# Softmax sums: turned by VectorE, written to DRAM in rows and read back for both heads at once, with a new instruction order

## The chip, the cores and the metric

The kernel runs on one core of a Trainium2 chip. The metric is device time in microseconds (us) of one execution, as the median of several runs.

## The reference

Attention with a threshold, for 4 batches, 8 heads, 576 queries and keys and a head width of 64, and behind it two feed-forward blocks over the 2304 resulting rows of 512:

```python
scores = (q @ k.T) / 8
thresh = max(scores) - tau                      # per query
scores = where(scores >= thresh, scores, -1e9) - max(scores)
attn = exp(scores)
attn = attn / (sum(attn) + 1e-9)                # one sum per query and head
x = (attn @ v) -> rows of 512                   # [2304, 512]
h = x @ w_in                                    # [2304, 2048]
g = (a0 + a1*h + a2*h**2 + a3*h**3) / (1 + |b0|*|h| + |b1|*h**2 + 1e-6)
y = g @ w_out                                   # [2304, 512]
out = ((y @ w1) * (y @ w2)) @ w3 @ w_out2       # [2304, 512]
```

## The kernel before

Two heads are worked on together as a pair: the 64 values of head 0 lie in partitions 0 to 63, those of head 1 in partitions 64 to 127. A unit of attention is a batch `b`, a pair `c` (0 to 3) and a half `u` of the queries: `u` = 0 is two blocks of 128 queries, `u` = 1 two more and the last 64 queries of both heads in one block (`blk` 4). There are 32 units. In a unit TensorE makes the scores (`qk`, L484 to L502), VectorE the maxima (`top`), ScalarE or VectorE the exponentials with their sums (`exp`), each block of probabilities is split into two 16-bit parts (`p_hi`, `p_lo`: tile `hl`) and transposed by a DMA (`p_t`, L584: `pT`, `pL`), and TensorE multiplies by the values (`pv`, L599).

The sums come out one per partition (one partition is one query), but they are needed along the free axis, because `pv` leaves the result with the queries along the free axis. So `recip` takes a unit's sums (tile `su`, 128 partitions by 4 or 5 columns: a column is a block and a head), adds 1e-9, takes the reciprocal (L552, L553, VectorE) and writes them to a buffer in DRAM, `d_r` (L555). `spread` reads them back, copied to 64 partitions for each head, into tile `R` (L563 for the 256 queries of both blocks, one DMA for each head; L567 for the 64 of `blk` 4, again one for each head). `x_split` (L610) and `x_tail` (L624) multiply the result of `pv` by `R`; this gives `xp` and `xl`, the input of the first feed-forward block.

That block (`mlp1`, tiles of 128 rows) runs `h_product` (L813), the rational function on ScalarE, VectorE and GpSimd (`act_h`, `num`, `den`, `inv`, `quotient`), a DMA transpose (`turn`, L865: `gt`) and `y_product` (L877). The second (`mlp2`) runs `ab_product` (L984), `c_mul`, a DMA transpose (`turn`) and `o_product` (L1013), and stores (`o_store`, L1025). Weights are loaded and split into 16-bit parts between (L675, `conv_w`, `split_w`).

All DMAs are issued by SyncE (SP), in one queue and in the order of the program. An instruction on SP that has to wait holds all that stand behind it. The order of the whole program is a written-out list, `ORDER`: each token is an event's number (a function call with its arguments; each time that it stands there the event goes on to its next `yield`), a letter for the engine of a step that can run on several (`a` ScalarE, `p` GpSimd, none or `v` VectorE), and the buffers that it takes. A planner outside the kernel made the list. Each engine works its part of the list strictly in order.

Of the kernel before, what the change touches and what calls it, by code (L numbers as in the profile page):

```python
# [10 lines left out]
F32 = mybir.dt.float32  # L11
# [5 lines left out]
ALU = mybir.AluOpType  # L17
# [14 lines left out]
0 5.0 1.1 3.2 12.0.1 19.2.3 2.0.0 7.1 4.1 13a 10.2 6.0 23.0.1 15.0 21p 25.0 8.1 27 22.1 9 29a.0  # L32
9.0 31.0.4 9 33.5 31v 11v.0.0 35a.6 33v 48.0.1 38p 17a.1.1 42p.7 40.0 11 44v 18.2 17 46.1 24.0
50.1 52 41.0 24 54v.1 24 56.8 86.4.0 20.1 34.1 58.1 20 56a 20 58a 90.0.1 60v.5 26.2 63v 73 65 43.2
67v.6 43 69v 73 43 71 92.2 88p 94 36.3 14.0 96v.2 36 98.1.7 36 100.8 152.1.5 28.4 98a 28 100a
115.0.1 28 75.0 108v.6 30.1 102p.3 37.2 117.3 119 104p 154a 121p.0 16.5 106.2 123.2 111v 125.7 16
123v 16 127a.8 32.6 45.0 125v 156.0.1 129p 140 140 39.7 32 39 131 32 39 49.1 159.0 134p.2 72.2 161
136p 163v.1 165.2.3 47.8 167.8 47 165a 47 167a 182.0.1 169p.7 59.0 51.9 171p 175p.3 53.1 51 74.10
51 74 62.1 61.11 74 53 61 81.2 177v 61 53 184.1 99.0 64.12 186 53 64 188p.2 190.0 64 192.4 77.0.0
190v 76.1 83a.2.2 55v.13 192v 219.0.1 113.0 194a.8 83 200a.6 101.14 80.1 173.1 79 101 79v 101  # L40
112.2 80 79v 116.0 78.15 138 196v 78 66.0 207 202p 221.2 207 198 223 66 78 225a.0 227.0.0 114.16
114 85.1 215.7.4 80 227v 114 118.17 89.2 66 118 232a.2 209.1 118 142.0 234v 80 230.8 598.0 230v 66
82a.18 238v.0 87.19 240v 107.1 87 217v 87 281 103.1 107 91.20 68v.21 244.0.1 91 93.0 91 246.3
# [12 lines left out]
332.6 273.1 636 280 352a 243 332v 243 334a.1 339 245p.0 251a.49 424.0 339 336p 424 356.0.1 264a.50
297.1 272a.51 424 253a.52 275 254a.53 424 253.0 275v 338.6 424 268a.54 275p 264.1 249a.55 358.3
274a.56 253v 341.1 260a.8 258v.9 251.0 280 264a 360 256a.10 249.1 304.2 251v 247a.11 319 361v.2
262a.15 254.0 249v 266a.12 260.1 270a.14 373.19 373 254v 363.2.7 260v 365.8 247.0 373 363a 306.20
256.1 284.0 365a 247v 306 266.0 256v 372p.1 378.0.1 306 266v 374p 311.2 444.0 380.0 381 268.1  # L60
286.23 383a.0 367v.4 387.5 286 272.0 387a 268v 426.1 286 272v 298.0 313.22 274.1 293.16 313 258.0
293 274v 426 258v 293 444 313 428.0 317.1 324.2 300.30 430 262.1 446.1 300 430 270.0 262v 400.1
385.8 385a 300 270v 331.0 302.1 443 448 375.0 320.17 428.1 448 428.0 320 347.1.1 376.0 433v 320
435 326.5 337.1 322.0 333.1 326 435 333 437.0 326 437 351.2 329.0 333 309.0 437 357.0 335.0 340.0
446.0 349 437p 401.1 446.1 461.1 349a 403p.1 340 439.0 405.3 353.4 276a.26 340 405a 353 344.1
343.0 450v 461 394a.1 359.3 452 353 445.0.1 452 359 364.2 355.1 455.1 342.1 359 315.1 455 377.0
463.0 346.6 455 466 349p 455v 466 457.1 366.24 346 379.7 346 379 664.1 348.1 366 362.0 379 282.1
366 431.0 463.0 423.2 447.2 463.0 449 289.1 468v 295.1 412 368.1 345.0 412 369v 470 345v 407v.6
370.2 382.1 345v 396v 470 384 389p.7 451a.2 398 384.1 508.0 453.0.5 409p 384 453a 414.0 386p.1
413a.2 399p.28 388a.40 508 411.3 417a.35 456a.4 410p.29 417.1 393p.36 276.0 417v 391v 440.1.6  # L70
388.1 472.0 392 454.8 276v 479.1 454a 390v.39 408a.33 406v.38 479 395v.43 388a 472 458v 410.0
481.1 472 481.1 390.1 442p 410v 510.0 483 472p 393.0 462a.5 512 481.1 390v 467.0.1 475.2 425.1.0
512 393a 441.1 483 510.0 427.2 469.3 510.0 420.1 460.1 486v 464v 488 395.0 471 514p 488 465.0 422
473v.0 636.0 416.1 395v 476.7 516.0.8 636 517 441 490.1 644a.41 422v 517 490 399.0 656a.46 476v
639p.0 650a.45 525.0 399v 484p.3 415a.37 418 490 642a.42 644.0 485v 419a.44 525 648a.24 422v 487
644v 490p 402a.47 397a.48 413.0 418p 492.0 418v 661a.6 489.1 653a.23 413v 404a.16 666.30 402.0
491.0 520 429.1 666 528.1 675.2 402v 658a.22 666 406.0 474.4 493v.1 686.1 530 669.1 474v 406a
672.1 495.5 530 404.0 518a 478v.7 495a 678.21 480v 522.0.1 678 482 404v 678 408.0 688.4 746.2
681.1 524.1 683 408a 688 432.1 397.0 502 688 502 434.0 526 696.1 397a 527v.2 529.1.2 648.0 529a
# [196 lines left out]
def tile_attention_mlps(  # L276
# [16 lines left out]
    nc = tc.nc  # L293
# [948 lines left out]
```

## Time and profile before

| | |
|---|---|
| median of 3 runs | 1327.58 us (1326.79 to 1328.59) |
| the profiled execution's own time | 1328.86 us |
| its span, from the first to the last instruction | 1327.1 us |
| mean granted clock of TensorE over the span | 0.911 of full speed |
| TensorE (PE) busy with matmuls | 1044.2 us, 79% |
| VectorE (DVE) busy | 874.2 us, 66% |
| ScalarE (ACT) busy | 584.1 us, 44% |
| GpSimd (POOL) busy | 339.2 us, 26% |

The own time is what the device counted for the profiled execution; the span is what its records cover, and the 1.8 us between the two lie outside of the instructions. Busy times are sums over the instructions of an engine. "SPq" is SyncE's sequencer, which issues the DMAs.

### The profile page before, as it was taken

Reading aid. Unit: us, or ns where it says so; the run is one execution under the profiler, and the core shown is the slowest. Engines: PE = TensorE matmul, PEld = TensorE weight load, DVE = VectorE, ACT = ScalarE, POOL = GpSimd, SP = SyncE. Lnnn points to the kernel's source line nnn. Section 1 sums busy time; section 2 is a strip of 40 time slices with the busy share of each in tenths; the row PEclk is TensorE's granted clock in tenths of the full one; section 3 lists DMA queues with packets and bytes.
Section 4 is the critical chain, followed back from the end, with each engine's and each line's share of the span. In section 5 each row is a group of like instructions: output and inputs, shape, how many; then the busy total and the mean of one; then the engine's idle time right before and its main releaser. Section 6 shows DMA issues by size and latency. Waiting matters only on the chain. (4 is left out here: it accounts for less than half of the span.)

```text
span 1327.1 us, 15744 instructions
## 1 busy us (share of the span) xinstructions
PE 1044.2 (79%) x5281; PEld 487.8 (37%) x5284; DVE 874.2 (66%) x1690; ACT 584.1 (44%) x1067; POOL 339.2 (26%) x353
## 2 busy tenths in 40 slices
PE   2388657577767969777798876787988989889998
PEld 1133323233323434343344333343434434444443
DVE  6566879877673767757575755675966754647652
ACT  4221365665642455453454544644643434425520
POOL 1201121211211333333331321253341423211210
PEclk9999778797888988898998897889998999999999
DMA  8789595675883868597578867477475445852333
GB/s 231 143 175 205 194 166 171 136 126 143 122 167 59 129 88 151 92 142 135 102 129 81 142 99 112 74 176 85 93 139 110 89 102 90 101 61 56 57 63 71
DMA packets 365345, 159.47 MB, mean 120 GB/s; under 512 B 329936, under 2 KB 342224, under 8 KB 365264
## 3 DMA queue, kind: packets, MB, share of 16 engines
q1 hardware_dynamic: 365264, 158.47, 65.3%
q8 instruction: 41, 0.67, 0.3%
q14 instruction: 40, 0.33, 0.1%
HBM read 74.71 MB, written 8.20 MB: 62 GB/s over the span
## 5 line engine op out<-in xcount | busy, mean ns | idle before, releaser
L877 PE MATMUL y<-wp,gt 128*128 128x512 f16 x864 | 221.3, 409 | 64.5 <-DMA gt<-gg 62.2
L813 PE MATMUL h<-wp,xp 128*128 128x512 f16 x768 | 185.1, 391 | 13.8 <-DVE R L610 10.1
L984 PE MATMUL h<-wp,yy 128*128 128x512 f16 x576 | 143.7, 400 | 24.4 <-DVE R L624 7.1
L877 PEld LDWEIGHTS <-gt 128*128 128x128 f16 x864 | 87.1, 104 | 189.1 <-DMA gt<-gg 71.8
L502 PE MATMUL S<-raw 64*128 64x288 f32 x512 | 101.2, 474 | 50.3 <-ACT p L539 18.5
L346 POOL TENSOR_TENSOR hl<-p,hl 128x576 f16<-128x576 f32 x71 | 99.4, 1403 | 140.7 <-ACT hl L330 68.0
L511 DVE TENSOR_REDUCE m<-S 128x1 f32<-128x576 f32 x144 | 104.1, 748 | 36.4 <-PE S L502 27.4
L813 PEld LDWEIGHTS <-xp 128*128 128x128 f16 x768 | 75.4, 100 | 112.1 <-issue 32.7
L1013 PE MATMUL y<-wp,gt 128*128 128x512 f16 x432 | 104.6, 390 | 9.4 <-DMA gt<-gg 9.4
L984 PEld LDWEIGHTS <-yy 128*128 128x128 f16 x624 | 62.5, 102 | 113.3 <-issue 43.2
L821 ACT ACTIVATE U<-h,cf 128x512 f32<-128x512 f32 x72 | 55.8, 775 | 88.4 <-PE h L813 45.0
L346 POOL TENSOR_TENSOR A<-A,r 128x512 f32<-128x512 f32 x40 | 52.8, 1321 | 156.1 <-ACT r L828 146.0
L534 ACT ACTIVATE S<-S,th 128x576 f32<-128x576 f32 x90 | 62.2, 711 | 68.3 <-DVE th L353 38.5
L502 PEld LDWEIGHTS S<-raw 64*128 64x128 f32 x512 | 55.3, 206 | 93.5 <-issue 44.0
L737 PE MATMUL y<-cw,dg 128*128 128x512 f32 x112 | 63.8, 653 | 29.4 <-DVE wp L334 20.3
L334 POOL CAST hl<-p 128x576 f16<-128x576 f32 x45 | 33.7, 751 | 189.2 <-DVE p L537 47.0
L346 POOL TENSOR_TENSOR gg<-A,r 128x512 f16<-128x512 f32 x37 | 51.7, 1397 | 116.6 <-DVE A L856 61.0
L346 DVE TENSOR_TENSOR hl<-p,hl 128x576 f16<-128x576 f32 x73 | 62.2, 854 | 22.0 <-POOL hl L334 13.9
L852 DVE SCALAR_TENSOR_TENSOR gg<-U,cf,r 128x512 f16<-128x512 f32 x72 | 55.8, 780 | 30.7 <-DMA gt<-gg 15.4
L833 DVE SCALAR_TENSOR_TENSOR U<-h,cf,U 128x512 f32<-128x512 f32 x72 | 53.6, 745 | 33.4 <-ACT r L828 23.4
L539 ACT ACTIVATE p<-S,xy 128x576 f32<-128x576 f32 x90 | 66.3, 742 | 19.8 <-DMA pT<-hl 16.8
L843 ACT ACTIVATE r<-A,lnb 128x512 f32<-128x512 f32 x72 | 51.7, 719 | 52.7 <-POOL A L346 32.1
(190 smaller groups left out, 1701.7 us busy)
## 6 DMA issues: line engine op xcount, KB each, us to landing
rw<-in_moe_w_dram SPq DMA_DIRECT2D x32, 512.0 KB, 4.5
rw<-in_moe_w_out_dram SPq DMA_DIRECT2D x24, 512.0 KB, 4.9
raw<-in_k_dram SPq DMA_DIRECT2D x32, 288.0 KB, 3.6
wr<-in_v_dram SPq DMA_DIRECT2D x16, 576.0 KB, 4.7
rw<-in_moe_w_in_dram SPq DMA_DIRECT2D x16, 512.0 KB, 3.5
wr<-in_v_dram SPq DMA_DIRECT2D x16, 320.0 KB, 4.6
R<-d_r SPq DMA_DIRECT2D x64, 64.0 KB, 3.7
out_dram<-A SPq DMA_DIRECT2D x16, 256.0 KB, 2.4
```

The source lines that it names most:

```text
L346: (nc.gpsimd if eng[0] == "p" else nc.vector).tensor_tensor(o, x, y, op=op)
L502: nc.tensor.matmul(t[s][:, half, :HS], x[r, o:o + 128], y[r, keys], start=True, stop=True)
L511: nc.vector.tensor_reduce(st["m", b, c, blk][:, s:s + 1], t[:, :, :HS], axis=AX.XY, op=ALU.max, negate=True)
L534: nc.scalar.activation(t, t, AF.Prelu, bias=th, alpha=BIG)
L539: nc.scalar.activation(x, t, AF.Exp, bias=xy[:, 0:1], accum_out=su)
L737: nc.tensor.matmul(y, st["dg", dg], r, start=True, stop=False)
L813: nc.tensor.matmul(t, x[:, y, c, o:o + 128], w[:, a, :], start=c + i == 0, stop=c == KD - 1 and i == 2)
L821: nc.scalar.activation(u, h, AF.Identity, bias=cf[:, 15:16], scale=cf[:, 0:1])
L852: stt(p[:, 0, :], u, cf[:, 3:4], r, ALU.add, ALU.mult)
L877: nc.tensor.matmul(st["y", n], x[:, 4 * a + j, :], w[:, y, :], start=f + j + i == 0, stop=f == 3 and j == 3 and i == 2)
L984: nc.tensor.matmul(t, x[:, 4 * y + c, :], w[:, a, :], start=c + i == 0, stop=c == KD - 1 and i == 2)
L1013: nc.tensor.matmul(st["o", n], x[:, 4 * a + j, :], w[:, y, :], start=hf + j + i == 0, stop=hf == 1 and j == 3 and i == 2)
```

## The change

After the reciprocal VectorE turns the unit's sums: `nc.vector.transpose` exchanges rows and columns inside each square block of 32 partitions by 32 columns. For that the sums live in one of three fixed tiles of 128 by 32 (`sums`, set to zero once), in place of a pool tile of 128 by 5. In the turned tile `sT` partition 32*i + k holds column k of the queries 32*i to 32*i + 31, so one partition holds 32 neighbouring queries. The write to `d_r` moves these rows of 32 values (128 bytes) where it moved single values (4 bytes); it writes all 32 columns, also those that hold no sums. The columns are numbered by head first, then by block, so that the 256 queries of one head are 1024 neighbouring bytes in `d_r`. The read for both heads is then one DMA (two with `blk` 4) in place of two (four).

The tile of ones, 128 by 128, becomes a column that is read with a stride of zero. `ORDER` is replaced by a new list. It holds the same 2440 events and, beside the reads of `R`, the same 514 DMA transfers; the reads of `R` are 48 where they were 96. Counted in the two lists, steps that can run on several engines moved so that VectorE has 29 fewer of them, GpSimd 21 more and ScalarE 8 more; the largest single groups are the last step of `quotient` (9 from VectorE to GpSimd), the second step of `exp` (11 from VectorE to ScalarE), the last step of `split_w` (18 from VectorE to ScalarE) and `p_hi` (16 more on VectorE). The list before and the list after put between a write of `d_r` and the read of the same unit in most units 0 to 4 other DMA issues.

```diff
 ORDER = """
...
-    d_r = [dr.tile([5 * 128], F32, name=f"d_r{j}") for j in range(2 * B * NP)]
+    d_r = [dr.tile([32 * 128], F32, name=f"d_r{j}") for j in range(2 * B * NP)]
...
+    c4 = cst.tile([128, 4], F32, name="c4")
+    d1, b1, unit = c4[:, 0:1], c4[:, 1:2], c4[:, 2:3]
...
-    ones = cst.tile([128, 128], F32, name="ones")
+    sums = [cst.tile([128, 32], F32, name=f"sums{j}") for j in range(3)]
...
-            st["su", b, c, u] = T("su", [128, 5])
+            st["su", b, c, u] = sums[(2 * (NP * b + c) + u) % 3]
         p = T("G", [128, S], name="p")
-        x, k = p.rearrange("p (j c) -> p j c", j=2), 2 * (blk - 2 * u) + s
+        x, k = p.rearrange("p (j c) -> p j c", j=2), 2 * s + blk - 2 * u if blk < 4 else 4
...
-        su, d = st.pop(("su", b, c, u))[:, :n], d_r[2 * (NP * b + c) + u]
-        nc.vector.tensor_scalar(su, su, 1e-9, None, op0=ALU.add)
-        nc.vector.reciprocal(su, su)
-        yield
-        nc.sync.dma_start(out=d[0:128 * n].rearrange("(k p) -> p k", p=128), in_=su)
+        su, d = st["su", b, c, u], d_r[2 * (NP * b + c) + u]
+        nc.vector.tensor_scalar(su[:, :n], su[:, :n], 1e-9, None, op0=ALU.add)
+        nc.vector.reciprocal(su[:, :n], su[:, :n])
+        t = T("sT", [128, 32])
+        nc.vector.transpose(t, su)
+        yield
+        nc.sync.dma_start(out=d.rearrange("(k i q) -> i k q", i=4, q=32), in_=t)
...
-        for s in range(2):
-            t = d[0:512].rearrange("(k h p) -> h k p", k=2, h=2)[s:s + 1]
-            nc.sync.dma_start(out=r[64 * s:64 * s + 64, 0:256].rearrange("p (k q) -> p k q", k=2),
-                              in_=t.to_broadcast([64, 2, 128]))
-            if u:
-                t = d[512 + 64 * s:576 + 64 * s].rearrange("(o q) -> o q", o=1)
-                nc.sync.dma_start(out=r[64 * s:64 * s + 64, 256:320], in_=t.to_broadcast([64, 64]))
+        t = d[0:512].rearrange("(h o q) -> h o q", h=2, o=1)
+        nc.sync.dma_start(out=r[:, 0:256], in_=t.to_broadcast([2, 64, 256]))
+        if u:
+            t = d[512:640].rearrange("(h o q) -> h o q", h=2, o=1)
+            nc.sync.dma_start(out=r[:, 256:320], in_=t.to_broadcast([2, 64, 64]))
...
-        nc.tensor.matmul(t, ones, vs[:, 3:4], start=True, stop=True)
+        nc.tensor.matmul(t, unit.to_broadcast([128, 128]), vs[:, 3:4], start=True, stop=True)
```

## Rows read from the trace of the kernel before

**Rows 1.** The page: its head, and busy time, share and instructions by engine.

```profile
span 1327.1 us, 15744 instructions
...
PE 1044.2 (79%) x5281; PEld 487.8 (37%) x5284; DVE 874.2 (66%) x1690; ACT 584.1 (44%) x1067; POOL 339.2 (26%) x353
```

**Rows 2.** Busy time by stretch: us, busy of each engine, PEclk, DMA share, GB/s.

```profile
27.84:1187.00 1159.16, 900.39 (x4611) 421.94 (x4614) 779.58 (x1515) 525.52 (x967) 311.44 (x320) 0.90 0.70 125
...
1187.00:1322.50 135.50, 134.61 (x646) 60.68 (x645) 78.98 (x137) 45.77 (x74) 21.80 (x18) 1.00 0.30 61
```

**Rows 3.** Waits of TensorE: us in total, times, longest us.

```profile
PE y L877 <- DMA gt<-gg: 62.2, 15, 7.9
...
PE h L599 <- DMA pT<-hl: 17.8, 6, 4.8
```

**Rows 4.** Waits of SyncE's queue: us in total, times, longest us.

```profile
SPq L563 <- DMA d_r<-su: 160.0, 24, 9.2
```

**Rows 5.** DMA issues, whole span: count, KB each, median us to landing.

```profile
raw<-in_k_dram SPq DMA_DIRECT2D x32, 288.0 KB, 3.6
...
R<-d_r SPq DMA_DIRECT2D x64, 64.0 KB, 3.7
out_dram<-A SPq DMA_DIRECT2D x16, 256.0 KB, 2.4
...
gt<-gg SPq DMA_TRANSPOSE x108, 3.2
R<-d_r SPq DMA_DIRECT2D x32, 16.0 KB, 2.9
...
d_r<-su SPq DMA_DIRECT2D x16, 2.0 KB, 9.9
d_r<-su SPq DMA_DIRECT2D x16, 2.5 KB, 9.8
```

**Rows 6.** Order of time on SyncE, 848 to 864 us: start us, us.

```profile
850.38 0.50 SPq L555 DMA_DIRECT2D d_r<-su  x1
851.55 1.24 SPq L865 DMA_TRANSPOSE gt<-gg  x1
860.80 0.61 SPq L563 DMA_DIRECT2D R<-d_r  x1
```

**Rows 7.** Order of time on TensorE, 848 to 872 us; idle before in brackets.

```profile
853.09 1.24 PE L502 MATMUL S<-raw 64*128 64x288 f32 x8
862.16 5.04 PE L877 MATMUL y<-wp,gt 128*128 128x512 f16 x12 [7.83 <-DMA gt<-gg]
```

**Rows 8.** DMA issues, 850.9 to 858 us and 591.5 to 597 us.

```profile
gt<-gg SPq DMA_TRANSPOSE x1, 10.6
...
out_dram<-A SPq DMA_DIRECT2D x1, 256.0 KB, 11.8
```

**Rows 9.** Busy time in 32 stretches of 15 us, each from an issue of L555.

```profile
27.84:42.84 15.00, 3.20 (x9) 1.81 (x8) 8.50 (x16) 2.81 (x6) 2.20 (x3) 1.00 0.69 114
...
1171.67:1186.67 15.00, 10.03 (x58) 5.17 (x57) 2.85 (x8) 0.69 (x2) 0.00 (x0) 0.89 0.86 68
sum 480.00, PE 314.91 PEld 146.94 DVE 253.46 ACT 171.34 POOL 110.77; mean PE 9.84 PEld 4.59 DVE 7.92 ACT 5.35 POOL 3.46
```

**Rows 10.** The chain that ended last: start us, us, what.

```profile
1125.11 9.46 DMA d_r<-su
...
1171.67 8.99 DMA d_r<-su
1180.66 0.02 issue
...
1181.98 4.38 DMA R<-d_r
```

**Rows 11.** Instructions on `d_r`: duration ns min/median/max, first and last start us.

```profile
L563 SPq DMA_DIRECT2D R<-d_r x64: 574/600/1277, 39.6 to 1182.0; - x64
```

**Rows 12.** Groups by line and shape: busy us, mean ns.

```profile
L346 POOL TENSOR_TENSOR gg<-A,r 128x512 f16<-128x512 f32 x37 | 51.7, 1397 | 116.6 <-DVE A L856 61.0 <-issue 17.0 <-PE y L1013 7.5
...
L346 DVE TENSOR_TENSOR gg<-A,r 128x512 f16<-128x512 f32 x35 | 27.5, 787 | 0.3
...
L553 DVE RECIPROCAL su<-su 128x5 f32<-128x5 f32 x16 | 3.0, 190 | 0.6
...
L728 DVE TENSOR_SCALAR dg<-ident,s 128x128 f32<-128x128 f32 x4 | 2.0, 488 | 0.0
```

More of the change, by code (lines that the diff above doesn't have):

```diff
@@ new lines @@
+390v.43 479 478v.7 495.5 410p.34 495v 390.1 502.0 481.0 480p 502 481.0 393.0 481.1 482 510.1
+522.0.1 483 486p 510.0 483 390a 504.1 420.0 514p 524.1 488 526 393a 517 441.1 527p.2 465.2 422 488
+422v 422v 517 410.0 529.0 519.1 636.1 529a 490.0 525.0 410v 533p.3 531.7 487 636 525 531a 490
+538a.1 648v.45 395.0 490 644a.47 519 528.0 416.1 490v 544.0.1 395a 418 639p.0 397a.36 530 441 540p
+429.0 546.2 530 434.0 644.0 492.0 418v 666.44 402a.42 642a.40 519 404a.8 666 542.0 644v 418p
+406p.48 658a.46 661a.22 547 415a.16 399.0 653a.5 549v.0 519p 399v 648.0 666 496v.4 516.8.2 553.7
@@ new lines @@
+719a 511p 572p 613.4 523.0 1103.1 721v 613a 511p 630.0.1 820.37 809.24 523 820 632.1 558 541 635
+622v.8 574.1 637p.0 809 541 820 809 856.0 823.0 773.1 625p 866.1 811.1 559 773v 615p.2 643.3
+594.5.4 643a 617p 814 826 559 826 619.2 640.6 828 828 576 640a 831p.1 834a.44 776v.19 576 660.0
+839v.20 660 869.17 836a.6 597v 834.1 579.1.0 869 579 679.1.0 781a.28 869 581a 585 878.1 682.2
+645a.2 662.0 834a 581 580.1 647p 776.1 685 583.2 687p.1 839.0 690.6 848.2 848 776a 690a 858.24 649
+836.1 848 839a 858 850.1 781.0 750.2 858 842a.13 836v 670.0 861.0 587 1124.0 881.14 781a 881
@@ new lines @@
+1047 1025.1 1073.0.1 974.1 1022v 1025 1363 964 1023.1 1009a.3 1010v 948 1068v.0 1367a.0 1075.3
+979p 1012 1076 948 964p 982 977 1078a.2 1365.1 982 1070v 966.2 1081.8 985.1 1365 1081a 985
+1049.2.7 1080.6 1093.1 985 1080a 1026.1 1370 985p 1028.0 1083a.4 1094.0 1006.1 1096p.0 1084v
+1097.3 1006 1370p.0 1086 1097a 1051v 1370p 969 1104.0 1008.1 1030 1104 1099p.5 1030a 1011 1088a.1
+1372.1 969 1030p 1120 1011 1101v 987.0 1031.0 1089v 1105.0 1122.0.1 1033 1033p 1072.0 1047.0 1374
+1047 1033p 1123.1 1115p.0.0 990 1125 1495.3 1126v.1 1495 1128.6 1102.4 990 1130.3 1495 1091 1128a
@@ new lines @@
+1184.1 1251 1184.0 1664 1064.2 1205v.4 1242v.2.2 1227v.7 1669a.1 1233 1186 1188p 1199.0 1253v.0
+1229p 1243.0.5 1190 1666.1 1190 1207p 1066 1234.0 1193.0 1254.1 1209.1 1666 1242 1254v 1245p
+1569.2 1066 1671 1176v 1193 1671a.1 1199 1176v 1193 1231 1256.4 1671p 1087 1202.0 1256v 1193p
+1202.0 1087 1202.1 1195.1 1204 1269.1.0 1206v 1673.2 1236.0.1 1204 1258p.7 1208 1271.3 1260p 1208
+1677.0 1273 1238 1262.0 1275p.1 1264v.2 1278.3 1677 1238v 1210.0 1090.1.1 1238v 1235.1 1210
+1682a.1 1278v 1265p 1263.0 1090 1210 1267.1 1092v 1263 1210p 1098 1092 1235 1213.0 1266.0 1695
@@ new lines @@
+1349.0 1226 1362.2 1349 1281 1338v.5 1228.1 1364 1340p 1699.0 1366v.1 1351.0 1368.3 1228 1357.7.2
+1688 1369.0 1228 1368a 1699 1228p 1283.0 1283.0 1688 1704 1283.1 1358a 1286 1288p 1704a.0 1299.0
+1230.2 1690v.1 1369a 1415 1286 1290 1299 1690 1704v 1290 1382.1.0 1301.1 1292.1 1279.0 1344a.6
+1384.3 1371a.8 1346v 1279 1301.1 1292 1348 1301.0 1386 1373p 1232 1303 1706.1 1388p.2 1292 1232
+1391.4 1303 1305p 1375.1 1390.3 1391v 1250 1292p 1308 1390v 1320.0 1317.1 1308 1404.1 1393v.6
+1294.2 1310.0 1317 1395v 1404 1310 1250 1397 1399p.8 1377a.3 1379p 1710.0 1342 1252.2.1 1252
@@ new lines @@
+1602.1.0 1553 1484.0.1 1508.0 1515.1 1484 1599p 1604.3 1606 1555.0 1601.1 1553v 1508 1608v.2 1553p
+1486v 1515 1612.4 1595.0 1491 1610.2 1486 1918 1612a 1556 1488.3 2412 1508 1517.0 1624.0 1556v
+1517.0 1508p 1517.1 1532.0 1626.1 1610a 1556p 1510.2 1519 1628p.1 1532 1613p.5 1519 1652.7.6
+1630.0 1656 1521p 1630v 1657.1.0 1493 1535.1 1637.0 1632p.1 1524 1537 1637 1513.1 1634p 1524
+1659.0 1654a 1661 1513 1615v 1663p.0 1619v.0 1617 1665.2 1573.1 1918 1526.1 1665a 1621v 1639.0
+1573 1920a.1 1550.1 1526 1844a.0.0 1920 1956.4 1623 1526 1550 1667.4 1956 1526p 1667a 1680.1.0
@@ new lines @@
+2027p 2294.1 1976 2048.1 2029 1887 2049 1999.1 2029 2051p.2 2054.4 2032.1 1999 2053.3 2054v 2053v
+2303.1 2295.0 2001.0 2032 2001.1 2032 2066.1 2001.1 2032p 2004 2295 2068.2 2006v 1996 2069p.0
+2071.5 2004 2009 2071v 1996 2061a.0 2021.1.6 2023v 2009 2063v 2305.1 2012.0 2064 2091 2305 2012
+2012 2092.0.1 2307a.1 2298v.0 2012v 2015.1 2050.0 2094.0 2014.2 2016 2096 2297.1 2016v 2097v.1
+2016p 2099.4 2297 2056a.0 2099v 2101.7 2058v 2017 2101v 1990a.3 2299 1992p 2017 2299p.0 1993
+2311.1 2073v.2 2299v 2311 2074p 2300.1 2050 2034.0 2313v.0 2306.1 2087.5.3 2306 2037 2089a 2308
@@ new lines @@
+2244 2260.1 2236 2245.0 2236 2245 2252.0 2237.1 2245 2260 2237 2245p 2252 2261.1 2237 2261.0 2362
+2261.1 2237v 2253.0 2262 2263p 2238.1 2371 2253.1 2262 2253.0 2371 2264 2254 2255p 2264 2254
+2276.1 2256 2256 2268.0 2276 2268 2265.1 2265 2265 2372v.1 2265p 2373 2425v.0 2425 2223.0 2223
+2231 2246.2 2231 2239 2266.0 2239 2247 2247 2376.0 2377 2377 2376 2373a.0 2373v 2364v.1 2365
+2365v.1 2365v 2366.1 2269.1 2269.0 2374.2 2269.1 2270 2271p 2270 2248.3.1 2272 2248 2257.0 2272
+2249v 2367 2257 2251 2257 2367 2383 2249 2277.0 2257p 2210.0 2250.1 2278 2375.0 2211 2278 2211v
@@ L272 @@
+2439
 """
@@ L307, in tile_attention_mlps @@
         w=57, gg=2, gt=3, xp=2, x4=4, dg=2, wr=3, U=2, A=2, r=2, G=9, pT=3, vh=4, vl=4,
[L308 removed]
+        R=2, m=4, th=3, sT=2, vs=2, sc=4, cf=6, xl=1,
     )
@@ L371, in tile_attention_mlps @@
     flag = cst.tile([128, 1], F32, name="flag")
-    d1 = cst.tile([128, 1], F32, name="d1")
+    c4 = cst.tile([128, 4], F32, name="c4")
+    d1, b1, unit = c4[:, 0:1], c4[:, 1:2], c4[:, 2:3]
     xy = cst.tile([128, 1], F32, name="xy")
@@ L396, in setup @@
         nc.sync.dma_start(out=bb, in_=cb.rearrange("(o c) -> o c", o=1).to_broadcast([128, 2]))
-        nc.gpsimd.memset(ones, 1.0)
+        nc.gpsimd.memset(unit, 1.0)
         nc.gpsimd.memset(onesh, 1.0)
+        for t in sums:
+            nc.gpsimd.memset(t, 0.0)
         nc.vector.tensor_scalar(flag, tau_t, 0.0, 0.125, op0=ALU.is_ge, op1=ALU.mult)
@@ L718, in scale_f @@
         t = P("h", [128, 512])[:, 0:1]
-        nc.tensor.matmul(t, ones, i[:, 3:4], start=True, stop=True)
+        nc.tensor.matmul(t, unit.to_broadcast([128, 128]), i[:, 3:4], start=True, stop=True)
         yield
```

433 lines of the change are left out of this document (191 added, 242 removed).

## The prediction

> **What bounds the kernel now.** I read the page's head first. TensorE is the busiest engine, yet 79% busy, with VectorE at 66%, ScalarE at 44% and GpSimd at 26% [rows 1]: no engine is full, so the time is TensorE's work plus the gaps in it. Busy time by stretch says where the gaps are. From 1187 us on TensorE is busy for 134.6 of 135.5 us at full clock; from 27.84 to 1187 us it is busy for 900.4 of 1159.2 us, so it idles for 258.8 us, at a mean clock of 0.90 [rows 2]. The end is therefore as good as full, and whatever the change is worth has to come out of those 258.8 us.
>
> What TensorE waits for is next. Its largest single wait is for the transposed input of the product in L877 (62.2 us), and that for `pT` is among the others (17.8 us) [rows 3]. Both are DMA transposes. SyncE's queue has one wait above all: L563, the read of `R`, waits for the write of `d_r`, 24 times, 160.0 us together [rows 4]. The table of DMA issues shows why: the write of 2 KB lands 9.9 us after its issue, a store of 256 KB after 2.4 us [rows 5].
>
> The wait on SyncE is the smaller part of it. At 850.38 us a write of `d_r` is issued, at 851.55 us, before any waiting, a transpose `gt`; SyncE then stands until 860.80 us [rows 6]. That transpose lands after 10.6 us, where the median of its kind is 3.2 us [rows 5, 8], and TensorE stands still for 7.83 us until 862.16 us for just this `gt` [rows 7]. Elsewhere a store of 256 KB, issued behind such a write, lands after 11.8 us in place of 2.4 us [rows 5, 8]. So what is issued behind a write of `d_r` lands only when that write is done: the write stops transfers, not only SyncE.
>
> To price that I took 32 stretches of 15 us, each from the issue of a write of `d_r`: the 9.9 us of the write and what follows at once. In their 480 us TensorE is busy for 314.9 us, so it idles for 165.1 us, 34% [rows 9]. The rest of the stretch from 27.84 to 1187 us has 679.2 us and 258.8 - 165.1 = 93.7 us of idling, 13.8%. At that rate the 480 us would hold 66.2 us. **The surplus is 98.9 us**, the ceiling of what TensorE's idling can give back through these writes. The chain that ended last agrees in kind: it runs through two of these writes, 9.46 and 8.99 us [rows 10].
>
> **The change part by part.**
>
> *The write of `d_r`.* It moves 128 pieces of 128 bytes in place of 512 or 640 of 4 bytes. No row shows such pieces. Below, 2.4 us: the store with 128 rows [rows 5]. Above, 9.9 us, if it is smallness itself that is slow. I take 3 us, near the store, since the number of rows is the same. With 640 pieces it takes no longer than with 512 (9.8 and 9.9 us [rows 5]), so I don't divide by the number of pieces. What goes is then about 9.9 - 2.4 = 7.5 us of stopped transfers per unit, at most 32 x 7.5 = 240 us, and nearly all of the 160.0 us on SyncE. As the lists leave 0 to 4 issues of other DMAs between write and read, at worst some 2 us of a wait remain where nothing stands between.
>
> *What TensorE gets of it.* Not the whole surplus. The stretches sit at the end of an attention unit, where probabilities are split, transposed and waited for in any case, and if a `gt` comes 7 us sooner, what is late next is the elementwise work that makes the next one: VectorE at 66% and GpSimd's long steps in front of it. From nothing (the gaps belong to the place, not to the write) to 98.9 us, I take half, **49.5 us**.
>
> *The clock.* A mean of 0.90 between the two levels of 1.2 and 2.4 GHz means a fifth of the 1159 us at the lower one, some 232 us [rows 2]. If idling falls by a fifth and the slow time with it (46 us, of which TensorE works 78% and half of that is lost), 18 us more come back. The 32 stretches are no slower than the rest (their rows begin at 1.00 and end at 0.89 [rows 9]), so I put nothing of it in the sum and keep it for the range.
>
> *The read of `R`.* 48 issues fewer on SyncE at 0.60 us [rows 11]: 29 us of a queue whose idle time hides it, except in the chain, where a read stands one or two issues earlier. Nothing in the sum. Its landing: below 2.9 us (the read of 16 KB), above 6.7 us (worked out under the second rival); I take 3.7 us, as the read with 64 partitions of two pieces has now [rows 5].
>
> *VectorE's turn.* 32 new instructions. The nearest rows are a reciprocal of 128x5 (0.19 us) and a scaling of 128x128 (0.49 us) [rows 12]: 6 to 16 us together on an engine that idles for a third of the time. Hidden by that, except 0.2 to 0.5 us on each unit's chain, which the 7.5 us cover. The fixed tiles of sums are used again after two units at the soonest; in the new list some 20 us of TensorE's work or more (an estimate, its matmuls counted at the full clock of the end [rows 2]) lie between a unit's reciprocal and the next first sum in its tile, so no wait. The column of ones and the zeroing at the start move nothing that lasts: nothing.
>
> *The order.* VectorE loses 29 steps of about 0.79 us (23 us), GpSimd gains 21 of about 1.40 us (29 us) [rows 12]. Neither becomes a bound: GpSimd goes from 339 to about 368 us of 1327 [rows 1]. But a step that moves is 0.61 us longer in its own chain: from nothing to 21 x 0.61 = 13 us. I take a third, **4 us**, as TensorE waits for only some of these chains.
>
> **Sum.** Against the profiled execution's own time, 1328.9 - 49.5 + 4 = 1283.4 us; the median of the runs lies 1.3 us lower, so 1282 us.
>
> **A rule that is weighed against the trace.** For the write, the row closest in place is the slow one itself, 9.9 us for pieces of 4 bytes [rows 5], and the closest in shape is the store with 2.4 us. The Trainium skill, in DMA: Bandwidth & Descriptors, section Specifications, says that pieces below 512 bytes are written by reading and changing what lies there; rows of 128 bytes are below that too. By that rule the write could stay as slow as it is, which is the first rival; no run here shows it.
>
> **The rivals.**
>
> *Small rows stay slow (0.08).* The write still takes 9.9 us at 128 bytes. For it: it doesn't depend on 512 or 640 pieces, so perhaps on the size below some limit. Against it: a piece grows 32-fold, and no row shows a limit above 4 bytes. Then only the 29 us of issues remain; at the surplus of 98.9 us per 480 us they are worth 6 us, and with the 4 us of the order it is 1328.9 - 6 + 4 - 1.3 = 1326 us: no change that shows.
>
> *The read of both heads runs on few engines (0.20).* Now each head's read spreads over 64 partitions; then the outermost count of the source is 2, the head. If a transfer is dealt out by that count, two of 16 engines carry 128 KB. 288 KB take 3.6 us, 1.2 us above the store's 2.4 us [rows 5]: 240 KB per us, 15 for each engine as an estimate. Half of 128 KB takes 4.3 us on each, landing at 6.7 us; the 32 KB of `blk` 4 take 1.1 us more in half of the units. All that needs those two engines waits: 16 x 4.3 + 16 x 5.4 = 155 of the 240 us come back as a new hold. Of the gain 85/240 remain, 17 us: 1328.9 - 17 + 4 - 1.3 = 1314 us. The trace has no DMA with so small an outer count, for or against. The Trainium skill states such a rule (DMA: Bandwidth & Descriptors, section Why a DMA increments its semaphore by 16 and not by 1): the number of engines is the largest up to 16 that divides the outermost counts of both sides, which here gives 2 for the read and 4 for the write. No run here shows it.
>
> *GpSimd's longer steps come last (0.14), slower.* Place: the last step of `quotient`, in front of the transpose `gt` that TensorE waits for most [rows 3]; price 0.61 us for a moved step, 13 us for all. It decides when the writes give back less than those 13 us, that is 13% of the surplus, as when the gaps belong to the end of a unit and not to the write. Then 1328.9 + 13 - 1.3 = 1341 us. Against it: `gt` in rows 6 and 7 was issued in time and late only in landing.
>
> **How the numbers follow.** The forecast has 0.58, its own range from 85% of the surplus (1248 us) to a quarter of it (1307 us); the rivals have 0.08, 0.20 and 0.14. The predicted time is 1282 us. For 8 in 10, I go from 1246 us, where some of the clock comes back too, to 1327 us, which leaves out the slower rival and a little at the lower end. Within 0.2% (2.7 us), about what a measurement of this kernel can tell from no change, is most of the first rival: 0.05. Faster is the forecast, nearly all of the second rival and a part of the first: 0.80. Slower is 0.15.
>
> **What would show it.** In the profile of the changed kernel: the write of `d_r` landing in about 3 us; SyncE's wait at L563 for it falling from 160 us to under 40; a `gt` issued right behind a write landing in 3 to 4 us; the read of `R` at about 3.7 us (6 us or more would speak for the second rival); TensorE's idling between the start and the last `x_split` falling from 259 to about 210 us. Wrong would be: the write lands fast and TensorE idles as long as before, then for VectorE or GpSimd; or the list costs more elsewhere than I allow.

## The result: 1144 us, and the profile after

The changed kernel takes 1144.24 us (median of 4 runs, 1141.80 to 1146.56) beside 1328.05 us for the kernel before in the same comparison: a ratio of 0.8617, 95% interval 0.8597 to 0.8637. That is 184 us less; the prediction had 1282 us, 46 us less, with a range that ended at 1246 us.

The page of the changed kernel, head and engine table:

```profile
span 1141.6 us, 15703 instructions
...
PE 1003.3 (88%) x5284; PEld 475.8 (42%) x5284; DVE 867.7 (76%) x1682; ACT 594.2 (52%) x1086; POOL 370.9 (32%) x377
```

Beside [rows 1] VectorE, ScalarE and GpSimd work about as long as before (GpSimd 32 us more, as the moved steps say). What shrank is the span around them, and TensorE's own busy time, by 41 us for the same work. Busy time by stretch, from the first write of `d_r` to the last `x_split`, and after it (columns as in [rows 2]):

```profile
29.93:998.00 968.07, 855.95 (x4573) 408.44 (x4573) 771.34 (x1499) 533.67 (x984) 340.11 (x336) 0.95 0.72 149
...
998.00:1136.00 138.00, 137.06 (x683) 62.04 (x683) 77.79 (x137) 47.05 (x76) 27.25 (x25) 1.00 0.31 63
```

The end is as full as it was [rows 2]. The first stretch went from 1159.2 to 968.1 us, by 191.1 us: TensorE's idling from 258.8 to 112.1 us (146.7 us) and its busy time from 900.4 to 856.0 us (44.4 us, with 38 matmuls fewer, which moved to the end), at a granted clock of 0.95 where it was 0.90. The stretches of 15 us from each write (29 of them, since those that overlap are joined), first, last and sum, as in [rows 9]:

```profile
29.93:59.92 29.99, 21.61 (x78) 10.69 (x78) 26.02 (x49) 12.89 (x27) 8.24 (x7) 1.00 1.03 237
...
989.10:1004.10 15.00, 13.36 (x83) 6.38 (x81) 7.17 (x12) 3.11 (x5) 4.39 (x5) 1.00 0.82 114
sum 463.92, PE 414.26 PEld 196.77 DVE 373.21 ACT 260.10 POOL 157.70; mean PE 14.28 PEld 6.79 DVE 12.87 ACT 8.97 POOL 5.44
```

TensorE idles for 49.7 of 463.9 us there, 10.7%, where it was 34%; in the rest of the stretch for 62.5 of 504.2 us, 12.4%, where it was 13.8%. The places behind a write are now no worse than others. They also hold 99 us more of TensorE's work than before, so a stretch of before and one of after are not the same work. TensorE's waits for transposes shrank with it ([rows 3] had 62.2 us for `gt` in L877, now L879; the wait for `pT` fell from 17.8 to 1.2 us):

```profile
PE h L705 <- ACT sq L696: 24.8, 12, 5.2
PE S L504 <- DVE p L539: 20.1, 5, 10.7
...
PE y L879 <- DMA gt<-gg: 8.1, 5, 2.1
```

SyncE's longest wait was for the write of `d_r`, 160.0 us [rows 4]. That wait is now 4.8 us (L566), and the longest are for GpSimd and VectorE:

```profile
SPq L867 <- POOL gg L346: 61.1, 20, 8.5
SPq L677 <- DVE cw L689: 52.3, 28, 6.5
```

The chain that ended last shows a write, and three reads of `R`:

```profile
607.67 1.98 DMA d_r<-sT
...
670.60 5.74 DMA R<-d_r
...
700.24 5.80 DMA R<-d_r
...
992.68 5.50 DMA R<-d_r
```

The write holds the chain for 1.98 us where [rows 10] had 9.46 and 8.99 us. The read takes 5.5 to 5.8 us: longer than the 4.38 us of [rows 10] and near the second rival's 6.7 us. The table of DMA issues prints no landing times for this kernel, so only these rows speak for its read and write; a kernel with landings follows below (b0).

### The profile page after: what moved, and what is told of

It reads as the page before. It is cut to its first block, busy times and chain, and to the rows that moved or that the text cites. A ratio compares the mean times of both kernels' runs of the same rounds, so it can differ in the third digit from the quotient of the medians.

```text
span 1141.6 us, 15703 instructions
## 1 busy us (share of the span) xinstructions
PE 1003.3 (88%) x5284; PEld 475.8 (42%) x5284; DVE 867.7 (76%) x1682; ACT 594.2 (52%) x1086; POOL 370.9 (32%) x377
## 4 chain that ended last, share of the span: by engine, by line
PE 45%; DVE 17%; DMA 10%; issue 4%; ACT 4%; POOL 2%; SPq 2%; DVEq 0%; ACTq 0%; POOLq 0%
PE y L879 9%; PE h L815 9%; PE h L986 6%; PE y L1015 6%; PE S L986 5%; DMA gt<-gg 3%; PE h L601 3%; PE S L504 3%; DVE m L513 2%; DMA pT<-hl 2%; PE y L739 2%; DMA raw<-in_q_dram 2%; DMA R<-d_r 1%; PE S L499 1%; DVE U L835 1%
## 5 line engine op out<-in xcount | busy, mean ns | idle before, releaser
L879 PE MATMUL y<-wp,gt 128*128 128x512 f16 x864 | 200.5, 382 | 9.2 <-DMA gt<-gg 8.1
L815 PE MATMUL h<-wp,xp 128*128 128x512 f16 x768 | 180.4, 383 | 8.5 <-ACT wp L330 2.2
L346 POOL TENSOR_TENSOR hl<-p,hl 128x576 f16<-128x576 f32 x76 | 107.7, 1419 | 167.3 <-ACT hl L330 69.3
L504 PE MATMUL S<-raw 64*128 64x288 f32 x512 | 104.2, 472 | 50.2 <-DVE p L539 20.1
L986 PE MATMUL h<-wp,yy 128*128 128x512 f16 x576 | 137.6, 385 | 6.3 <-DVE U L837 3.1
L879 PEld LDWEIGHTS <-gt 128*128 128x128 f16 x864 | 83.4, 98 | 116.5 <-DMA gt<-gg 11.3
L1015 PE MATMUL y<-wp,gt 128*128 128x512 f16 x432 | 103.4, 387 | 7.7 <-DMA gt<-gg 6.6
L346 POOL TENSOR_TENSOR gg<-A,r 128x512 f16<-128x512 f32 x46 | 60.8, 1323 | 137.6 <-DVE A L858 93.2
L536 ACT ACTIVATE S<-S,th 128x576 f32<-128x576 f32 x101 | 70.4, 709 | 63.3 <-DVE th L353 42.8
L541 ACT ACTIVATE p<-S,xy 128x576 f32<-128x576 f32 x101 | 74.7, 742 | 10.4 <-DMA pL<-hl 6.3
L1015 PEld LDWEIGHTS <-gt 128*128 128x128 f16 x432 | 41.9, 100 | 61.2 <-DMA gt<-gg 8.4
L936 PE MATMUL h<-cw 128*128 128x512 f32 x128 | 62.3, 638 | 5.4 <-DVE cw L334 3.6
```

What stands on the lines that cost most here:

```text
L346: (nc.gpsimd if eng[0] == "p" else nc.vector).tensor_tensor(o, x, y, op=op)
L504: nc.tensor.matmul(t[s][:, half, :HS], x[r, o:o + 128], y[r, keys], start=True, stop=True)
L536: nc.scalar.activation(t, t, AF.Prelu, bias=th, alpha=BIG)
L541: nc.scalar.activation(x, t, AF.Exp, bias=xy[:, 0:1], accum_out=su)
L815: nc.tensor.matmul(t, x[:, y, c, o:o + 128], w[:, a, :], start=c + i == 0, stop=c == KD - 1 and i == 2)
L879: nc.tensor.matmul(st["y", n], x[:, 4 * a + j, :], w[:, y, :], start=f + j + i == 0, stop=f == 3 and j == 3 and i == 2)
```

## The experiments

Each was timed in turns with the kernel before. These comparisons ran on other chips, where the kernel before takes 1340 to 1344 us, so ratios to it are compared. All compute what the kernel computes; b1 to b5 write something besides. The names of the theories are those of e1's expectation: the path is the way of the sums (turn, write, read), the order is the list.

**Path and order apart.** e1 has the new turn, write and read with the list of before; a unit's tile of sums is the one whose place the old list names:

```diff
-ORDER = """ (new list) """
+ORDER = """ (list of before) """
-            st["su", b, c, u] = sums[(2 * (NP * b + c) + u) % 3]
+            st["su", b, c, u] = sums[places.pop(0)]
```

> The changed kernel's turn, write and read, with the order of the kernel before; the full computation. Path theory (the writes of 4-byte pieces that stop all transfers cost nearly all of the 184 us, the new order adds under 20 us): 1150 to 1180 us. Order theory (the path is worth the 50 us of the prediction, the order the rest): 1265 to 1295 us. Pair theory (the order before was laid around the slow write, so each is worth half without the other): 1210 to 1250 us.

Measured: 0.8707 (0.8672 to 0.8743), 1168.1 us, as the path theory had it. e2 is the opposite, the new list with the old write and a read for each head:

```diff
-        t = T("sT", [128, 32])
-        nc.vector.transpose(t, su)
+        places.clear()
         yield
-        nc.sync.dma_start(out=d.rearrange("(k i q) -> i k q", i=4, q=32), in_=t)
+        nc.sync.dma_start(out=d[0:128 * n].rearrange("(k p) -> p k", p=128), in_=su[:, :n])
...
-        t = d[0:512].rearrange("(h o q) -> h o q", h=2, o=1)
-        nc.sync.dma_start(out=r[:, 0:256], in_=t.to_broadcast([2, 64, 256]))
+        for s in range(2):
+            t = d[256 * s:256 * s + 256].rearrange("(o q) -> o q", o=1)
+            nc.sync.dma_start(out=r[64 * s:64 * s + 64, 0:256], in_=t.to_broadcast([64, 256]))
...
```

(and the same for the 64 queries of `blk` 4). The columns stay numbered by head, so each head's read takes 256 neighbouring values, where the kernel before reads two runs of 128; it lands after 3.6 us, as before (3.7 us [rows 5]).

> The new order with the write in 4-byte pieces and the reads for each head by itself, as before; the full computation. Path theory: 1310 to 1335 us. Order theory: 1185 to 1215 us. Pair theory: 1240 to 1300 us.

Measured: 0.991 (0.9879 to 0.994), 1326.4 us. The list alone is worth about 1%. Order theory and pair theory fall.

**Write and read apart.** e3 takes only the first part of e2's edit (the write), e4 only the second (the reads).

> The changed kernel with only the write of the sums put back to 4-byte pieces (and no turn); the read for both heads stays; the full computation. If the write is what matters of the path, as e2 within 10 us in every theory; if the read for both heads has a share, between the changed kernel and e2.

Measured: 1.036 (1.0318 to 1.0403), 1387.1 us: not e2 but 61 us slower than it, and slower than the kernel before. What all the theories left out is a cost of the read for both heads. In its chain stand two writes in 4-byte pieces, 12.07 and 9.52 us, and a read of 6.43 us; e2's chain has seven such writes, 7.98 to 19.14 us, and reads of 3.07 and 2.99 us.

> The changed kernel with only the read put back to one DMA (two with the last block) for each head, 64 partitions each; the full computation. If the read for both heads runs on few engines and that costs: landing 3 to 4 us in place of 5.4 to 5.8 us and 1125 to 1140 us. If the halved number of issues is worth more: 1147 to 1160 us. If the read hardly matters: 1140 to 1148 us.

Measured: 0.8224 (0.8192 to 0.8256), 1102.8 us. The read for both heads costs, and more than expected: 0.8617/0.8224 is 1.048, some 50 us. With the read for each head by itself the changed kernel beats both; this is the fastest version found. Its page:

```profile
span 1102.6 us, 15795 instructions
...
PE 991.9 (90%) x5284; PEld 472.4 (43%) x5284; DVE 872.8 (79%) x1682; ACT 593.7 (54%) x1086; POOL 372.1 (34%) x377
```

e5 is e1's list with e4's read, which leaves of the whole change the write alone, with the turn and the fixed tiles that it needs.

> The kernel before, its order and its reads for each head kept, with the turn and the write in rows of 128 bytes alone; the full computation. If order, write and read add up as e1 to e4 say (write in rows -15 to -17%, few-engine read +4%, order -1%): 0.83 to 0.84 of the kernel before, 1110 to 1130 us. If the order before needs its slow write: over 1160 us.

Measured: 0.8412 (0.8391 to 0.8433), 1129.9 us, a little above the expected ratio of 0.84. So the write alone, with the list and the reads of before, brings 15.9%, 211 us of 1328 us: more than the whole change. The combinations, as ratios to the kernel before ("old read" is a read for each head; in the kernel before itself, of two runs each):

| | old read, old list | new read, old list | old read, new list | new read, new list |
|---|---|---|---|---|
| old write | 1 | not run | 0.991 | 1.036 |
| new write | 0.8412 | 0.8707 | 0.8224 | 0.8617 |

Write: -15.9% (old list), -17.0% and -16.8% (new list). Read for both heads: +3.5%, +4.5%, +4.8%. List: -0.9%, -2.2%, -1.0%.

**Why the read costs.** e8 keeps both heads in one DMA but cuts it by queries, so that it has e4's number of issues:

```diff
-        t = d[0:512].rearrange("(h o q) -> h o q", h=2, o=1)
-        nc.sync.dma_start(out=r[:, 0:256], in_=t.to_broadcast([2, 64, 256]))
+        for s in range(2):
+            t = d[0:512].rearrange("(h o q) -> h o q", h=2, o=1)[:, :, 128 * s:128 * s + 128]
+            nc.sync.dma_start(out=r[:, 128 * s:128 * s + 128], in_=t.to_broadcast([2, 64, 128]))
...
```

> The changed kernel with the read cut in two by queries, both heads in each DMA, so that it has as many issues, bytes and pieces for each DMA as e4's read, but the outermost count of the source stays 2; the full computation. Theory that the outermost count deals the transfer to few engines: no faster than the changed kernel, 0.86 to 0.88 of the kernel before. Theory that the size of the single transfer or the number of issues made the difference: as e4, 0.82 to 0.83.

Measured: 0.8566 (0.8525 to 0.8607), 1148.1 us: nearly the changed kernel, far from e4. It doesn't match e4 in all else: it has 128 pieces of 512 bytes in a DMA where e4 has 64 of 1024, but the changed kernel's read, with pieces of 1024 bytes, is as slow. In its chain a read still takes

```profile
673.67 4.47 DMA R<-d_r
...
701.66 4.64 DMA R<-d_r
...
996.01 4.90 DMA R<-d_r
```

with half of the bytes in each. So neither the number of issues nor the size of one transfer makes the difference. What the changed kernel and e8 share is the outermost count of 2, the head.

The packets of the queue tell what that count does. The lines of the changed kernel, of e4 and of e8, one fence each:

```profile
q1 hardware_dynamic: 345008, 158.91, 66.7%
```

```profile
q1 hardware_dynamic: 346448, 158.92, 63.9%
```

```profile
q1 hardware_dynamic: 351248, 158.91, 63.9%
```

e4 moves the same 6144 pieces of `R` as the changed kernel, in 96 DMAs where that has 48, and shows 1440 packets more. That is 96 x 16 - 48 x 2. e8 has 96 DMAs too and 6144 pieces more, since they are half as long, yet only 4800 packets more than e4: 6144 - 96 x 14. Both come out exactly if a DMA adds one packet for each engine that carries it, 16 engines for e4's reads and 2 for the reads of both heads. This is worked out from the counts; that a read of both heads fills 128 partitions and not 64 was not varied by itself.

**What a write of 4-byte pieces costs by itself.** b0 is e4 with the write cut into four DMAs of 32 partitions, so that no transfer has a small outermost count; its profile prints all landings:

```diff
-        nc.sync.dma_start(out=d.rearrange("(k i q) -> i k q", i=4, q=32), in_=t)
+        for i in range(4):
+            x = d.rearrange("(k i q) -> i k q", i=4, q=32)[i]
+            nc.sync.dma_start(out=x, in_=t[32 * i:32 * i + 32, :])
```

> The changed kernel with the reads of e4 (one DMA for each head) and the write split into four DMAs of 32 partitions each, so that the outermost count of no transfer is small; the full computation. It is the base for the next three, and shows the landing times that the changed kernel's profile doesn't print. If dealing the write out over more engines matters: under 1095 us beside e4's 1103. If only the three more issues on SyncE count: 1103 to 1112 us. Landing of each write 2.0 to 2.5 us in either case.

Measured: 0.8334 (0.8301 to 0.8366), 1116.0 us. By the ratios it is 1.3% slower than e4, some 15 us: more than the issues were expected to cost, and no gain from more engines for the write. That there are more engines the packets tell again: 348368, which is 1920 more than in e4, or 128 x 16 - 32 x 4. Its DMA table, columns as in [rows 5]:

```profile
R<-d_r SPq DMA_DIRECT2D x64, 64.0 KB, 2.7
...
d_r<-sT SPq DMA_DIRECT2D x128, 4.0 KB, 1.6
gt<-gg SPq DMA_TRANSPOSE x108, 3.2
R<-d_r SPq DMA_DIRECT2D x32, 16.0 KB, 2.5
```

In its chain a read takes 2.44 to 2.61 us, where the changed kernel's takes 5.5 to 5.8 us:

```profile
612.72 2.56 DMA R<-d_r
```

To b0 the next five add one write for each unit, of the sums to a spare buffer `d_x`, that nothing waits for. b1: 512 pieces of 4 bytes side by side, as the kernel before writes them.

```diff
+        x = d_x[2 * (NP * b + c) + u].rearrange("(k p) -> p k", p=128)
+        nc.sync.dma_start(out=x, in_=su[:, :4])
```

> b0 and, behind each unit's write, a second write of the unit's four columns of sums in 512 pieces of 4 bytes to a spare buffer in DRAM that nothing reads or waits for; the full computation and this besides. Theory that the stop of all transfers is the cost: 32 stops of some 7.5 us, and with TensorE at 90% nearly all of it is lost: 150 to 220 us more than b0. Theory that the wait on SyncE for the write was the cost: under 40 us more, since nothing waits for this one.

Measured: 1.0226 (1.0165 to 1.0286), 1370.9 us: 255 us more than b0's 1116.0 us in the same comparison, 8.0 us for each write. That is beyond the range expected of the stop, and far from the other theory's. TensorE's row on its page, and the two lines of its DMA table:

```profile
PE 1048.8 (77%) x5284; PEld 490.6 (36%) x5284; DVE 863.7 (63%) x1682; ACT 594.3 (43%) x1086; POOL 363.2 (27%) x377
```

```profile
R<-d_r SPq DMA_DIRECT2D x64, 64.0 KB, 10.1
...
d_x<-sums SPq DMA_DIRECT2D x32, 2.0 KB, 10.3
```

The extra write lands after 10.3 us, and the reads of `R` behind it, which need nothing from it, after 10.1 us in place of 2.7 us. TensorE's busy time is 1048.8 us, within 5 us of the kernel before's [rows 1], though its work is b0's (997.4 us there). By stretch, from the first of these writes to the end of attention and in the joined stretches of 15 us from each (columns as in [rows 2] and [rows 9]), b1 first, then b0, where the stretches begin at the write of `d_r`:

```profile
32.47:1222.70 1190.23, 900.26 (x4567) 422.62 (x4568) 764.77 (x1494) 532.41 (x982) 332.14 (x336) 0.88 0.69 121
...
sum 467.40, PE 270.81 PEld 125.14 DVE 221.14 ACT 163.41 POOL 95.02; mean PE 8.74 PEld 4.04 DVE 7.13 ACT 5.27 POOL 3.07
```

```profile
30.08:970.30 940.22, 850.35 (x4573) 406.83 (x4573) 771.66 (x1500) 533.74 (x984) 339.04 (x336) 0.96 0.68 153
...
sum 463.53, PE 423.36 PEld 200.75 DVE 382.18 ACT 260.44 POOL 164.84; mean PE 14.11 PEld 6.69 DVE 12.74 ACT 8.68 POOL 5.49
```

With the extra writes TensorE idles for 290.0 us, without them for 89.9 us: of the 255 us, 200.1 us are idling and 49.9 us are busy time in this stretch.

b2 writes one column (128 pieces of 4 bytes), b3 the four columns with each piece 64 bytes from the next, b4 the four columns as 128 pieces of 16 bytes side by side, b5 as b3 with 16 bytes from one piece to the next (the lines are shortened):

```diff
+b2     x = d_x[...].rearrange("(k p) -> p k", p=128)              # from su[:, :1]
+b3     x = d_x[...].rearrange("(k p z) -> p k z", p=128, z=16)[:, :, 0]
+b4     x = d_x[...].rearrange("(p k) -> p k", p=128)
+b5     x = d_x[...].rearrange("(k p z) -> p k z", p=128, z=4)[:, :, 0]
```

> As b1 with one column: 128 pieces of 4 bytes. If the stop goes with the number of pieces: a landing of 3.5 to 4.5 us and 30 to 55 us more than b0. If a write of such pieces has a fixed stop: a landing of 9 to 10 us and as much as b1.

> As b1 with each 4-byte piece 64 bytes from the next in DRAM, in place of side by side. If pieces that lie side by side hinder one another in the memory: a landing under 4 us and under 30 us more than b0. If the number of pieces or their size alone counts: as b1 within 20 us.

> b0 and an extra write of the four columns as 128 pieces of 16 bytes, side by side in DRAM, to a spare buffer that nothing reads or waits for. If pieces that share 64 bytes of DRAM hinder one another in proportion to how many share them (4 here, 16 in b2): a landing of 3 to 5 us and 30 to 70 us more than b0. If any sharing stops everything: a landing of 8 to 10 us and 180 to 220 us more. If only 4-byte pieces do it: as b3, 15 us more.

> As b3 with each 4-byte piece 16 bytes from the next, so that four of them share 64 bytes of DRAM, as the 16-byte pieces of b4 do. If sharing 64 bytes is what hinders: a landing of 8 to 10 us and 150 to 250 us more than b0. If pieces have to lie closer than 16 bytes: as b3, a landing near 2 us and about 15 us more than b0, and what b4 showed holds for small pieces too.

Measured: b2 0.9868 (0.9822 to 0.9914), b3 0.8444 (0.8401 to 0.8487), b4 0.8484 (0.8449 to 0.8518), b5 0.8471 (0.8432 to 0.8511). The line of the extra write in the DMA table of b2, of b3, of b4 and of b5, one fence each:

```profile
d_x<-sums SPq DMA_DIRECT2D x32, 0.5 KB, 9.0
```

```profile
d_x<-sums SPq DMA_DIRECT2D x32, 2.0 KB, 2.1
```

```profile
d_x<-sums SPq DMA_DIRECT2D x32, 2.0 KB, 1.5
```

```profile
d_x<-sums SPq DMA_DIRECT2D x32, 2.0 KB, 3.1
```

A quarter of the pieces, side by side, still takes 9.0 us and costs 18% over b0 (by the ratios, some 205 us). All 512 pieces of the same 4 bytes, spaced, take 2.1 or 3.1 us and cost 1.3% and 1.6% (15 and 18 us), and 16-byte pieces side by side 1.5 us and 1.8% (20 us); one more issue for each unit is in all of these. The pieces are what the edits say: b1, b3 and b5 show 365264 packets in the queue, b2 and b4 352976, which is 512 and 128 for each extra write and 16 more. b4 fits the last of its three cases, near b3. b5 lands 1 us later than b3, far below the 8 to 10 us of its first case. So neither the number of pieces nor their size makes the write slow, nor that four of them share 64 bytes. It is slow when 4-byte pieces lie directly side by side. Whether they have to touch, or whether more than four to 64 bytes are enough, was not run (nothing between 4 and 16 bytes of distance was), and what in the memory or the transfer does it stays open.

## Why the prediction was wrong: the right cause at a quarter of its size

- **What the write stops.** Right in its effect, and it was the point: what is issued behind a write of `d_r` lands late. b1 shows it alone, without any wait for the write. What is held, the trace of before tells more closely than the prediction did. Around the `gt` of [rows 6], from 850 to 864 us in 40 slices of 0.35 us, the busy tenths of the DMA engines and the GB/s that they move are:

```profile
DMA  5999930099955000000000000000000000004313
GB/s 109 217 210 186 125 3 0 20 213 212 203 101 23 0 0 0 0 0 0 0 0 0 0 0 0 0 0 0 0 0 0 0 0 0 0 13 114 90 30 88
```

  The data of this `gt`, issued at 851.55 us, have moved by 854.6 us. From there to 862.2 us the engines move nothing, SyncE stands [rows 6], and only then `gt` lands (10.6 us after its issue). So at this place the write doesn't keep the engines busy: what it holds is the landing, and with it all that waits for one. The new write lands after 1.6 us in b0 and holds a chain for 1.98 us, where 3 us were taken; 9.9 - 1.6 = 8.3 us go, where the sum had 7.5 us.
- **What TensorE gets of it: the step that failed.** The prediction called the surplus of 98.9 us a ceiling and took half of it, 49.5 us, since the next wait would take the rest. Measured, TensorE's idling fell by 146.7 us. No other engine was near its limit to take the wait over: VectorE now works 76% of the span, where it had 66%, for about the same work, and in e4 TensorE reaches 90%. Nor is the surplus a ceiling. It set the idling elsewhere, 13.8%, against the length of the stretches, but these shrink when idling goes: the 314.9 us of work in them would take 365 us at that rate, with 50.4 us of idling, and the surplus is 114.7 us. And b1 and b0 test the method itself. b1 idles for 196.6 of its 467.4 us behind the extra writes and for 93.4 of 722.8 us (12.9%) elsewhere, so the prediction's sum gives a surplus of 136 us; b0 shows that 200.1 us of idling go, and 49.9 us of busy time besides. A part of the difference lies behind the 15 us: from 15 to 20 us after a write (or to the next one) TensorE idles for 29% of the time in b1 and for 11% in b0. In the kernel before that can't be seen (19%, and 18% after the change), so where its other 32 us come from stays open. In b1, 8.0 us of time for each write stand beside 10.3 - 2.1 = 8.2 us by which it lands later than the spaced one, in b2 some 6.4 us beside 6.9 us: a price of nearly 1 for each us that landings are held. At that price, which only these runs gave, the 240 us that the prediction itself counted were the size to forecast; the write alone brought 211 us (e5).
- **The clock.** Left out of the sum, with at most 18 us. Measured: TensorE's busy time fell by 40.9 us over the span, at a granted clock of 0.95 in the first stretch where it was 0.90. In b1 it is the other way, 997.4 us in b0 and 1048.8 us with the extra writes. What failed is the reading that the stretches behind a write are no slower than the rest. Over the 32 rows of 15 us the mean is 0.90, as elsewhere, but the row averages over a drop: in the first 10 us from an issue of L555 the mean granted clock is 0.97, in the next 10 us 0.78, and below 0.90 in 26 of the 32. In the changed kernel these two are 0.99 and 0.95. The two rows behind the write of [rows 6]:

```profile
850.38:860.38 10.00, 3.95 (x21) 1.77 (x19) 7.53 (x17) 7.34 (x14) 2.11 (x3) 0.81 0.32 52
860.38:870.38 10.00, 7.96 (x28) 3.26 (x30) 2.89 (x14) 1.97 (x3) 0.35 (x1) 0.68 0.60 162
```

  TensorE first idles for 6 of 10 us, and the next 10 us have a granted clock of 0.68, while it works for 8 of them. Between the levels of 1.2 and 2.4 GHz, 0.78 in these 320 us means that some 144 us of them are at the lower one, of the 232 us that the prediction counted in all (an estimate from these rows). The way of the term was right. What went in was too small: it took a fifth less idling, and idling fell by 57%, which in the same working gives 51 us.
- **The read for both heads.** The second rival held, beside the forecast and not in its place: 5.5 to 5.8 us in the chain was nearer to its 6.7 us than to the 3.7 us taken, and the cost is some 50 us (the changed kernel against e4; 61 us from e2 to e3), where the rival's time lay 32 us over the forecast, as it took its share of a gain that was itself too small. The rule in the Trainium skill (DMA: Bandwidth & Descriptors, section Why a DMA increments its semaphore by 16 and not by 1), that the outermost counts decide how many engines carry a transfer, agrees with e8 (4.47 to 4.90 us for half the bytes, nearly the same time), with b0 (2.7 us, both counts 64) and with the packet counts, which give 2 engines for the read and 4 for the write; which engines these were no view here tells.
- **The order.** 4 us of loss were taken; it is a gain of 0.9% to 2.2% (12 to 25 us). GpSimd's longer steps, the slower rival, don't show: TensorE waits 8.1 us for the first block's `gt` where it waited 62.2 us [rows 3]. Its case fails.
- **Small rows stay slow**, the first rival, fails: rows of 128 bytes land in 1.6 us. The rule on pieces below 512 bytes (the Trainium skill, DMA: Bandwidth & Descriptors, section Specifications) doesn't tell such a write from the slow one; here even 4-byte pieces at a distance land in 2.1 us.
- **VectorE's turn** was estimated at 6 to 16 us of work and put at nothing. Its row in the changed kernel has 6.8 us:

```profile
L557 DVE STREAM_TRANSPOSE sT<-sums 128x32 f32<-128x32 f32 x32 | 6.8, 212 | 1.1
```

  With the list of before (e1) VectorE is busy for 879.8 us beside 874.2 us [rows 1], in 32 more instructions. What the turn and the fixed tiles cost in time no run tells apart; e5 has them, and its 211 us are what is left after them.

## What to carry to other kernels

When one short DMA lands late, look at what was issued behind it before asking who waits for it. If that lands late too, count the time for which landings are held at nearly its full length, as it was here, where the busiest engine waited for transfers and no other engine was close behind. A row that averages over a stop hides what follows it: cut the stretch behind the stop in two before saying that the clock is no lower there. Write to DRAM in rows, not in single 4-byte values side by side. Give a large read an outermost count that is large, even if that takes one more issue; for the small write, with a count of 4, the same cure cost 1.3% (b0). Measure the parts of a change apart: here the read took back a quarter of what the write brought, and the whole still looked like a success.

## What the runs showed of the hardware

- A write of 4-byte pieces that lie side by side in DRAM lands in 9.0 us with 128 pieces and 10.3 us with 512; the same 512 pieces 64 bytes apart land in 2.1 us, 16 bytes apart in 3.1 us, and 128 pieces of 16 bytes side by side in 1.5 us.
- What is issued behind such a write lands after it, also transfers that have nothing to do with it: reads of `R` after 10.1 us in place of 2.7 us (b1), a store after 11.8 us in place of 2.4 us [rows 5, 8]. For one transpose the trace of before shows that its data had moved 7.6 us before it landed, and that no engine moved anything in between. The Trainium skill (DMA: Bandwidth & Descriptors, section Queues, rings and completion order) says that the signal of a finished transfer lands only after every earlier write of its DMA engine; these rows agree.
- A read of 128 KB whose outermost count is 2 takes 5.5 to 5.8 us in the chain of the changed kernel (5.17 to 7.97 us in e1's). The same bytes as two reads with an outermost count of 64 land in 2.7 us each, 2.44 to 2.61 us in the chain (b0). The packet counts of the queue differ as if 2 engines carried the first and 16 the second (e4, e8).
- Where TensorE idles behind a slow write, its granted clock is lower afterwards: 0.97 in the first 10 us from the issue of a write and 0.78 in the next 10 us, before the change; 0.99 and 0.95 after it.
